# Two chunks' keys as a seven-product pair, and the loads reordered to suit, in a gated attention + GEGLU kernel

## The chip, the cores and the metric

The kernel runs on one core of one Trainium2 chip. The metric is the device time of one execution in microseconds (us). Engines are named as in the profile: PE is TensorE's matmul stream, PEld its weight loads, DVE is VectorE, ACT is ScalarE, POOL is GpSimd, SP is SyncE, which here only issues DMA transfers.

## The reference, cut to what matters

```python
# x: 2048 x 1024, wqkv: 1024 x 3072, wo: 1024 x 1024, w_gate and w_up: 1024 x 3584, w_down: 3584 x 1024, bf16
qkv = x @ wqkv                                  # 32 heads of 32
# every row attends to itself and 7 rows behind it, 2 apart
a = softmax(q . k[rows] / sqrt(32)) @ v[rows] @ wo
b = (gelu(x @ w_gate) * (x @ w_up)) @ w_down
g = sigmoid((x * gate_w).sum(-1))
out = g * a + (1 - g) * b
```

## The kernel before: the parts that matter here

The 2048 rows are four chunks of 512. Chunks 0 and 1 are the first half (`sup == 0`), chunks 2 and 3 the second. Each half does queries, keys and values, then the feed-forward network (FFN), then the two down projections. The attention of a half runs on DVE while PE is in the FFN.

Most products are "seven-product pairs", a Strassen-like scheme: a 2 x 2 block product takes seven block matmuls instead of eight. DVE pays for it with sums and differences of weight blocks ("forms") and with additions behind the products. In the kernel before, of the first half's queries, keys and values only the values are such a pair. Queries and keys of chunks 0 and 1 are plain: eight tiles of eight matmuls per chunk.

```python
def main():                                     # the order of work on PE
    ...                                         # transposes of chunk 0's input
    yield from qkv_outer(0)                     # queries of chunk 0
    yield from qkv(0, 1)                        # keys of chunk 0
    yield from gate(0)
    yield from qkv_pair(0, [2])                 # values of chunks 0 and 1: seven products
    yield from gate_sum(0)
    yield from qkv(1, 0)                        # queries of chunk 1
    yield from qkv(1, 1)                        # keys of chunk 1
    yield from gate(1)
    yield from halo(1)
    for sup in range(NSUP):
        ...                                     # ffn, down, then the second half's pair

def loads():                                    # the order of loads, all issued by SP
    ...                                         # query weights, eight loads
    yield from load_qkv(0, 1, range(KT))        # key weights
    yield Op("SP", ...)                         # value weights
    yield from load_x(1, [])                    # chunk 1's input, eight transposing loads
    yield load_prep(0)                          # blocks of w_down for the down projection's forms
    yield load_prep(2)
    yield from load_block(0, 0)                 # FFN weights
    ...
```

The order of instructions on each engine is fixed while the program is written. A planner holds a modelled clock per engine and one for the DMA pipe, and always emits next the operation that its model can start first. Each stream of operations has a bias, and some operations have a due time before which the bias counts.

```python
class Weave:
    LAT = 0.1
    RATE = 340e3                                # bytes per us
    AHEAD = 11.0
    ...
    def _emit(self, op, t):
        ...
        if op.eng in ("SP", "POOL", "ACTQ"):    # a DMA
            nbytes, issue = op.cost
            self.clk[self.home(op)] = t + issue
            self.pipe = max(self.pipe, t) + nbytes / self.RATE
            op.end = self.pipe + 2.2 + ...
        else:
            self.clk[op.eng] = t + cost
    ...
            b = s[0] if op.due is None or t + self.AHEAD < op.due else 0.0
            if best is None or t + b < best[0]:
                best = (t + b, t, s, op)

w.run([(0.0, main()), (0.0, loads()), (0.0, late_x()), (0.88, wforms()), (0.0, down_forms()), (0.1, x_forms()),
       (1.43, qkv_forms()), (1.3, preps()), (0.13, attention()), (0.36, scores())])
```

Every DMA byte costs the planner the same, whatever the size of the packets it travels in.

Of the kernel before, what the change touches and what calls it, by code (L numbers as in the profile page):

```python
# [30 lines left out]
class Op:  # L31


    def __init__(self, eng, cost, fn, deps=(), key=None, table=None, pre=None, lag=0.0, tail=0.08, kind=None, after=False, due=None):
        self.eng, self.cost, self.fn, self.deps, self.key = eng, cost, fn, deps, key
        self.table, self.pre, self.lag, self.tail = table, pre, lag, tail
        self.kind = kind
        self.after, self.ins = after, None
        self.due = due
        self.end = None  # L40


class Weave:
# [7 lines left out]
    AHEAD = 11.0  # L51
# [76 lines left out]
    def run(self, streams):  # L128
# [5 lines left out]
        while live:  # L134
            best = None
            for s in live:
                op = s[2] if isinstance(s[2], Op) else s[2]()
                t = None if op is None else self._start(op)
                if t is None:
                    continue  # L140
                b = s[0] if op.due is None or t + self.AHEAD < op.due else 0.0
                if best is None or t + b < best[0]:
                    best = (t + b, t, s, op)
# [9 lines left out]
def kernel(  # L153
# [63 lines left out]
    DUE = (88.5, 308.0)  # L217
# [33 lines left out]
    def bank_take():  # L251
        best = min(range(len(bank_free)), key=lambda i: -1.0 if bank_free[i][1] is None else bank_free[i][1].end)
        return bank_free.pop(best)

    def bank_give(i, op):
        bank_free.append((i, op))

# [37 lines left out]
    warm = hrow[:, XR + NST, 0:SC]  # L295
    nc.vector.memset(warm, 0.0)
    for i in range(5):
        nc.tensor.matmul(banks[7][:], lhsT=warm[:, 0:P], rhs=warm, start=True, stop=True)
# [27 lines left out]
    def load_qkv(c, which, order=range(KT), deps=()):  # L326
        for kt in order:
            yield ring_load(("wqkv", c, which, kt), lambda g, kt=kt: nc.sync.dma_start(
                out=g.rearrange("p (k n) -> p k n", k=1), in_=qkv_src(which, kt, 1)), deps)

# [60 lines left out]
    def loads():  # L391
        for kt in range(KT):
            yield Op("SP", (P * D * 2, 0.45), lambda kt=kt: nc.sync.dma_start(
                out=qbuf[:, kt:kt + 1], in_=qkv_src(0, kt, 1)), key=("wqkv", 0, 0, kt))
        yield from load_qkv(0, 1, range(KT))
        yield Op("SP", (KT * P * D * 2, 1.0), lambda: [nc.sync.dma_start(out=vbuf[:, hf * KH:(hf + 1) * KH],
                                                                        in_=qkv_src(2, hf * KH, KH)) for hf in range(2)],
                 [("pt", NST - 1, 1)], key=("wqkv", 0, 2))
        yield from load_x(1, [])
# [24 lines left out]
    def preps():  # L424
        for i0 in range(0, NPREP, 2):
# [5 lines left out]
            f0 = dve(t, lambda: V(out=b11, in0=b12, in1=b11, op=ALU.subtract), due=DUE[0] + 4.0 * i0, deps=[("prep", i0), ], lag=1.0)  # L431
            yield f0
            yield dve(t, lambda: V(out=b12, in0=b22, in1=b12, op=ALU.subtract), due=DUE[0] + 4.0 * i0)  # L433
            f1 = dve(t, lambda: V(out=b22, in0=b22, in1=b11, op=ALU.subtract), [f0], due=DUE[0] + 4.0 * i0)
            yield f1
            last = dve(t, lambda: V(out=b21, in0=b21, in1=b22, op=ALU.subtract), [f1], due=DUE[0] + 4.0 * i0)
# [33 lines left out]
    def x_forms():  # L470
        t = tt(KH * SC)
        for sup in range(NSUP):
# [4 lines left out]
            t1 = dve(t, lambda b12=b12, b11=b11: V(out=tf[:, 0], in0=b12, in1=b11, op=ALU.subtract), dx + free, lag=1.0, key=("xf", sup, 1))  # L477
            yield t1
            t2 = dve(t, lambda b22=b22: V(out=tf[:, 1], in0=b22, in1=tf[:, 0], op=ALU.subtract), [t1], key=("xf", sup, 2))
            yield t2  # L480
            yield dve(t, lambda b12=b12, b22=b22: V(out=b12, in0=b22, in1=b12, op=ALU.subtract), [("z", c0)], key=("xf", sup, 3))  # L481
            yield dve(t, lambda b21=b21: V(out=tf[:, 2], in0=b21, in1=tf[:, 1], op=ALU.subtract), [t2], key=("xf", sup))
# [22 lines left out]
    def qkv(c, which):  # L505
# [3 lines left out]
        for t in range(NT):  # L509
# [11 lines left out]
        if c == 1 and which == 1:  # L521
            for kt in range(KT):
                ring_give(("wqkv", 0, 1, kt), o)

    def qkv_outer(c):
        taken = [bank_take() for t in range(NT)]
        for kt in range(KT):
# [8 lines left out]
            else:  # L536
                o = pe(NT, go, d)
                yield o
        for t in range(NT):
            i = taken[t][0]  # L540
            if t % 2 == 0 or c:
# [11 lines left out]
    def qkv_forms():  # L553
        for sup in range(NSUP):
            c = 2 * sup
            t = tt(D // 2)
            for which in QVK if sup else (2,):
                def raw(kt, hi, which=which, c=c):
                    return qkv_w(c, which, kt).rearrange("p (m t) -> p m t", t=NT)[:, :, KH * hi:KH * hi + KH]

                def form(f, kt, which=which, c=c):
                    return ring[:, held["wqf", c, which, f, kt // 2], kt % 2 * D // 2:(kt % 2 + 1) * D // 2] \
                        .rearrange("p (m t) -> p m t", t=KH)

                for f in range(4):
                    for kt in range(KH):
                        if True:
                            def go(f=f, kt=kt, which=which, c=c):
                                if f != 2 and kt % 2 == 0:
                                    ring_take(("wqf", c, which, f, kt // 2))  # L570
                                o, x_, y_, op = ((lambda: form(0, kt), lambda: raw(kt, 1), lambda: raw(kt + KH, 1), ALU.add),
                                                 (lambda: form(1, kt), lambda: form(0, kt), lambda: raw(kt, 0), ALU.subtract),
                                                 (lambda: raw(kt, 1), lambda: raw(kt, 0), lambda: raw(kt, 1), ALU.subtract),
                                                 (lambda: form(3, kt), lambda: raw(kt + KH, 0), lambda: form(1, kt),
                                                  ALU.subtract))[f]
                                V(out=o(), in0=x_(), in1=y_(), op=op)  # L576
                            dep = raw_keys(c, which, (kt, kt + KH))
                            if f in (1, 2):
                                dep.append(("wq", c, which, 0, kt))
                            elif f == 3:  # L580
                                dep.append(("wq", c, which, 1, kt))
                            yield dve(t, go, dep, key=("wq", c, which, f, kt), lag=0.5,
                                      pre=ring_pre if (f != 2 and kt % 2 == 0) else None,
                                      due=DUE[1] + 23.0 * QVK.index(which) + 2.5 * f if sup else 0.0)
# [20 lines left out]
    def qkv_pair(c, whichs=QVK):  # L605
# [35 lines left out]
        for which in whichs:  # L641
            for g in range(2):
                ts = (2 * g, 2 * g + 1)
                A, Bk, Dk, m5, u2 = {}, {}, {}, {}, {}
                for t in ts:
# [3 lines left out]
                    Bk[t], fr = bank_take()  # L649
# [103 lines left out]
    def gate_sum(c):  # L753
# [13 lines left out]
        bank_give(i, e)  # L767
# [14 lines left out]
    def scores():  # L782

        for c in range(NCH):
            q_, k_ = qo[c % 2], kT[c]
            for a in range(SC // AC):
# [15 lines left out]
                def add(t):  # L802
                    def fn():
                        V(out=w3(box[0]), in0=w3(box[0]), in1=w3(box[t]), op=ALU.add)  # L804
                    return dve(tt(n), fn, [last["m", t], last["acc"]], key=("qk", h) if t == NT - 1 else None, kind="a")

                todo, pend = list(range(NT)), []
# [27 lines left out]
    def att_half(c, a, h):  # L835
# [112 lines left out]
        def s4(t):  # L948
            return flat(("s", t // 2)).rearrange("p (u w s) -> p u w s", u=2, w=4)

        def sums(t, m):
            def fn():
                V(out=s4(t)[:, t % 2], in0=w3(box["p", t])[:, 0:4], in1=w3(box["p", t])[:, 4:8], op=ALU.add)  # L953
            return dve(tt(n // 2), taking(("s", t // 2), fn) if t % 2 == 0 else fn, [m],
                       pre=xb_pre() if t % 2 == 0 else None)
# [9 lines left out]
        for t in range(0, NT + 2, 2):  # L965
            for u in range(2):
# [3 lines left out]
                if t:  # L970
                    if u == 0:
                        f = fold2(t - 2, [ss[t - 2], ss[t - 1]])
                        yield f
                    else:
                        f = fold1(t - 2, f)
                        yield f
                        xb_give(box["s", (t - 2) // 2], f)
                        if a and t == NT:
                            w.done["att", c] = f
            if t < NT:  # L980
                for u in range(2):
                    ss[t + u] = sums(t + u, ms[t + u])
                    yield ss[t + u]
                    xb_give(box["p", t + u], ss[t + u])
# [3 lines left out]
    def ffn(sup, mid, early=()):  # L988
# [29 lines left out]
        for i in range(FT + 2):  # L1018
            if i < FT:
# [3 lines left out]
                Bk[f], fr = bank_take()  # L1023
# [303 lines left out]
```

## Time and profile before

| before | value | from |
|---|---|---|
| time, median | 725.16 us | timed runs |
| span of the profiled execution | 723.8 us | page, first line |
| PE busy | 713.6 us, 99% | page, part 1 |
| DVE busy | 598.5 us, 83% | page, part 1 |
| DVE busy from 40 to 300 us | 246.57 us, 94.8% | windows |
| waits of PE, in sum | about 3 us | waits of PE |

The head of the page of before: the span, and each engine's busy time with its share of the span and its number of instructions.

```profile
span 723.8 us, 9915 instructions
...
PE 713.6 (99%) x3314; PEld 351.1 (49%) x3381; DVE 598.5 (83%) x898; ACT 315.3 (44%) x535; POOL 71.8 (10%) x128
```

The waits of PE in before: what waited, what it waited for, us in total, times, longest.

```profile
PE ps L298 <- DVE hT L296: 1.2, 1, 1.2
PE ps L1252 <- DMA hT<-in_A_x_dram: 0.5, 1, 0.5
PE ps L628 <- DVE lend L481: 0.5, 1, 0.5
PE ps L995 <- ACT m L1049: 0.4, 1, 0.4
PE ps L496 <- DVE lend L1259: 0.3, 1, 0.3
```

PE is full. The first wait is before the real work starts. From the first query matmul on, PE stands for about 1 us in the whole kernel. So this kernel gets faster only if PE gets less to do, or by that 1 us.

The timeline of PE in before, at the borders of the stages: start, length, operation, and in brackets an idle time ahead of it with its releaser.

```profile
7.02 13.97 PE L496 MATMUL ps<-lend,hT 128*128 128x512 bf16 x62 [0.29 <-DVE lend L1259]
...
88.11 1.04 PE L995 MATMUL ps<-lend,ring 128*128 128x512 bf16 x4
...
312.65 1.05 PE L735 MATMUL ps<-lend,gcol 128*32 128x512 bf16 x16
...
441.66 1.03 PE L995 MATMUL ps<-lend,ring 128*128 128x512 bf16 x4
```

These are four clock readings: queries start at 7.02, the first FFN at 88.11, the second half's gates at 312.65, the second FFN at 441.66. Their differences are the stage lengths.

### The profile page before, as it was taken

Reading aid. Unit: us, or ns where it says so; the run is one execution under the profiler, and the core shown is the slowest. Engines: PE = TensorE matmul, PEld = TensorE weight load, DVE = VectorE, ACT = ScalarE, POOL = GpSimd, SP = SyncE. Lnnn points to the kernel's source line nnn. Section 1 sums busy time; section 2 is a strip of 40 time slices with the busy share of each in tenths; the row PEclk is TensorE's granted clock in tenths of the full one; section 3 lists DMA queues with packets and bytes.
Section 4 is the critical chain, followed back from the end, with each engine's and each line's share of the span. In section 5 each row is a group of like instructions: output and inputs, shape, how many; then the busy total and the mean of one; then the engine's idle time right before and its main releaser. Section 6 shows DMA issues by size and latency. Waiting matters only on the chain.

```text
span 723.8 us, 9915 instructions
## 1 busy us (share of the span) xinstructions
PE 713.6 (99%) x3314; PEld 351.1 (49%) x3381; DVE 598.5 (83%) x898; ACT 315.3 (44%) x535; POOL 71.8 (10%) x128
## 2 busy tenths in 40 slices
PE   8999999999999999999999999999999999999997
PEld 5666644444444444455665444444444444444443
DVE  1799999999999899799599976999999995794200
ACT  2353465557655532035552114567558557110110
POOL 1000433343121100100000000000000000001000
PEclk9999999999999999999999999999999999999999
DMA  9944799989989979945239999786566657999992
GB/s 313 236 149 103 222 354 318 334 256 349 267 218 193 274 239 299 344 143 146 58 97 300 362 324 309 236 186 177 157 178 159 177 157 178 313 326 331 327 304 99
DMA packets 180931, 172.12 MB, mean 238 GB/s; under 512 B 56464, under 2 KB 137360, under 8 KB 180880
## 3 DMA queue, kind: packets, MB, share of 16 engines
q1 hardware_dynamic: 172048, 143.69, 68.5%
q0 software_dynamic: 8544, 27.27, 10.7%
q8 instruction: 26, 0.43, 0.2%
q10 hardware_dynamic: 288, 0.52, 0.2%
q14 instruction: 25, 0.20, 0.1%
HBM read 129.50 MB, written 28.31 MB: 218 GB/s over the span
## 4 chain that ended last, share of the span: by engine, by line
PE 83%; DVE 8%; DMA 4%; issue 4%; POOL 1%; ACT 0%; DVEq 0%; POOLq 0%; ACTq 0%
PE ps L995 35%; PE ps L1159 28%; PE ps L628 12%; PE ps L496 8%; DMA fforms<-ring 1%; DVE ring L457 1%; DVE ring L576 1%; DVE hT L1058 1%; DMA ring<-in_B_w_down_dram 1%; DMA ring<-in_A_wqkv_dram 1%; DMA hT<-in_A_wo_dram 1%; DMA hT<-in_B_w_down_dram 1%; DVE hT L1120 1%; DVE hT L1039 1%; DVE hT L433 0%
## 5 line engine op out<-in xcount | busy, mean ns | idle before, releaser
L995 PEld LDWEIGHTS <-ring 128*128 128x128 bf16 x1568 | 153.2, 98 | 185.8 <-issue 1.6
L995 PE MATMUL ps<-lend,ring 128*128 128x512 bf16 x877 | 210.5, 379 | 1.3 <-ACT m L1049 0.4
L995 PE MATMUL ps<-tf,ring 128*128 128x512 bf16 x659 | 162.6, 379 | 0.7
L1159 PE MATMUL ps<-ring,hT 128*128 128x512 bf16 x696 | 159.7, 379 | 0.6
L1159 PEld LDWEIGHTS <-hT 128*128 128x128 bf16 x708 | 69.2, 98 | 83.3
L945 DVE TENSOR_TENSOR xbuf<-xbuf,lend 128x2048 bf16<-128x2048 bf16 x64 | 77.4, 1215 | 7.5 <-DMA xbuf<-xbuf 7.5
L798 DVE TENSOR_TENSOR xbuf<-qo,lend 128x2048 bf16<-128x2048 bf16 x64 | 76.7, 1216 | 0.1
L804 DVE TENSOR_TENSOR xbuf<-xbuf 128x2048 bf16<-128x2048 bf16 x56 | 68.2, 1217 | 0.3
L628 PEld LDWEIGHTS <-ring 128*128 128x128 bf16 x384 | 49.3, 129 | 34.4 <-DVE lend L481 0.9
L1024 ACT COPY ps<-ps 128x512 f32<-128x512 f32 x56 | 32.0, 571 | 55.6 <-PE ps L995 55.5
L1067 ACT ACTIVATE gl<-ps 128x512 bf16<-128x512 f32 x56 | 33.5, 598 | 49.6 <-PE ps L995 48.5
L1194 ACT ACTIVATE ost<-ps,omg 128x512 bf16<-128x512 f32 x16 | 11.0, 688 | 100.6 <-PE ps L1159 81.9
L1186 POOL DMA_DIRECT2D out_dram<-ost x24 | 13.0, 540 | 411.0 <-ACT ost L1194 319.1
L1159 PE MATMUL ps<-ring,qo 128*128 128x512 bf16 x187 | 48.5, 379 | 0.2
L466 POOL DMA_DIRECT2D fforms<-ring x56 | 30.6, 546 | 175.3 <-DVE ring L457 166.1
L628 PE MATMUL ps<-lend,ring 128*128 128x512 bf16 x203 | 47.0, 380 | 0.7 <-DVE lend L481 0.5
L1039 DVE TENSOR_TENSOR hT<-hT,gl 128x1024 bf16<-128x1024 bf16 x56 | 38.3, 683 | 11.3 <-ACT hT L1036 11.3
L953 DVE TENSOR_TENSOR xbuf<-xbuf 128x1024 bf16<-128x1024 bf16 x64 | 42.0, 683 | 0.4
L1079 DVE TENSOR_TENSOR u<-ps,u 128x512 f32<-128x512 f32 x56 | 38.3, 684 | 4.6 <-PE ps L995 3.2
L628 PE MATMUL ps<-tf,ring 128*128 128x512 bf16 x173 | 40.1, 379 | 0.2
L1058 DVE TENSOR_TENSOR hT<-ps,m 128x512 bf16<-128x512 f32 x56 | 38.2, 683 | 1.5 <-PE ps L995 1.4
L1075 ACT COPY u<-ps 128x512 f32<-128x512 f32 x56 | 32.9, 587 | 15.1 <-PE ps L995 15.1
(110 smaller groups left out, 697.1 us busy)
## 6 DMA issues: line engine op xcount, KB each, us to landing
ring<-dforms SPq DMA_DIRECT2D x112, 256.0 KB, 5.3
ring<-in_B_w_down_dram SPq DMA_DIRECT2D x84, 256.0 KB, 4.6
ring<-in_B_w_gate_dram SPq DMA_DIRECT2D x56, 256.0 KB, 4.8
fforms<-ring POOLq DMA_DIRECT2D x56, 256.0 KB, 5.3
ring<-fforms SPq DMA_DIRECT2D x56, 256.0 KB, 4.0
ring<-in_B_w_up_dram SPq DMA_DIRECT2D x42, 256.0 KB, 4.7
ring<-in_A_wqkv_dram SPq DMA_DIRECT2D x32, 256.0 KB, 5.4
ring<-oforms SPq DMA_DIRECT2D x32, 256.0 KB, 5.7
```

The lines of the kernel that those rows point to most:

```text
L496: nc.tensor.matmul(banks[bk][:], lhsT=lhsT, rhs=xT(c, kt), start=(kt == 0), stop=(kt == KT - 1))
L628: nc.tensor.matmul(banks[bk][:], lhsT=lhsT, rhs=rhs[:, kt, :], start=(start and kt == 0), stop=(kt == KH - 1), skip_group_check=True)
L798: V(out=w3(box[t]), in0=q_b, in1=k_w, op=ALU.mult)
L804: V(out=w3(box[0]), in0=w3(box[0]), in1=w3(box[t]), op=ALU.add)
L945: return dve(tt(n), taking(("p", t), lambda: V(out=w3(box["p", t]), in0=w3(box["ab"]), in1=v_w, op=ALU.mult)), [("qkv", c, 2, t), abo] + ( ...
L953: V(out=s4(t)[:, t % 2], in0=w3(box["p", t])[:, 0:4], in1=w3(box["p", t])[:, 4:8], op=ALU.add)
L995: nc.tensor.matmul(banks[bk][:], lhsT=wv[:, k, fl * P:(fl + 1) * P], rhs=rhs[:, k, :], start=(start and k == 0), stop=(k == KH - 1), skip_ ...
L1039: yield dve(tt(2 * SC), lambda f=f: nc.vector.tensor_tensor(out=hrow[:, f, :], in0=hrow[:, f, :], in1=gl[f][:], op=ALU.mult), [e, ev[f, "g ...
L1058: ev[f, "up2"] = dve(tt(SC, True), lambda f=f: nc.vector.tensor_tensor(out=hs(f, 1), in0=v3(banks[Bk[f]][:]), in1=v3(m5[f][:]), op=ALU.add ...
L1067: nc.scalar.activation(out=gl[f][:, SC:2 * SC], in_=banks[A[f]][:], func=ACT.Gelu_apprx_tanh)
L1079: e = dve(tt(SC, True), lambda f=f: nc.vector.tensor_tensor(out=u2[f][:], in0=banks[Dk[f]][:], in1=u2[f][:], op=ALU.add), [o, ev[f, "u2"]])
L1159: nc.tensor.matmul(banks[bk][:], lhsT=l, rhs=wv[:, i, :], start=(start and k == 0), stop=(q == last and i == 1), skip_group_check=True)
```

## The change

The intent: keys of chunks 0 and 1 also become a seven-product pair, which takes 16 of 128 matmuls away. A pair needs the input of both chunks, so chunk 1's input is wanted sooner. Three query tiles of chunk 1 are put ahead of the pair, to give the key weights time to land. Chunk 1's transposing loads are issued from ACT's queue, the key weights from POOL behind the sixth of them, and the value weights last. With this went a retuned planner (due times, biases), forms and attention sums merged into fewer, wider instructions, a longer warm-up and some smaller changes (input forms that wait for half of the loads, the order of score sums, the choice of PSUM banks). The core of the diff:

```diff
-    AHEAD = 11.0
+    AHEAD = 17.53
...
+    NFILL = 3
-    DUE = (88.5, 308.0)
+    DUE = (99.8, 308.54)
...
-    for i in range(5):
-        nc.tensor.matmul(banks[7][:], lhsT=warm[:, 0:P], rhs=warm, start=True, stop=True)
+    for n_ in [SC] * 6 + [P] * 3:
+        nc.tensor.matmul(banks[7][:, 0:n_], ...)
...
+    def early_x():                              # chunk 1's input, issued from ACT's queue
+        for kt in range(KT):
+            yield Op("ACTQ", (P * SC * 2, 1.3), lambda kt=kt: nc.scalar.dma_start_transpose(
+                out=xT(1, kt), in_=x[SC:2 * SC, kt * P:(kt + 1) * P]), [("pt", NST - 1, 1)], key=("x", 1, kt))
+    def early_k():                              # key weights, issued from POOL after x(1, 5)
...
     def loads():
-        yield from load_qkv(0, 1, range(KT))
-        yield from load_x(1, [])
...
     def preps():                                # forms of the down weights; prep block i0
-            f0 = dve(..., due=DUE[0] + 4.0 * i0, ...)
+            f0 = dve(..., due=DUE[0] + 4.84 * i0, ...)
...
     def qkv_forms():                            # one instruction now takes two weight rows
-            t = tt(D // 2)
-            for which in QVK if sup else (2,):
+            t = tt(D)
+            for which in QVK if sup else (1, 2):
                 def raw(kt, hi, which=which, c=c):
-                    return qkv_w(c, which, kt).rearrange("p (m t) -> p m t", t=NT)[:, :, KH * hi:KH * hi + KH]
+                    w0, w1 = qkv_w(c, which, kt), qkv_w(c, which, kt + 1)
+                    return _win_ap(w0[:, KH * hi:KH * hi + 1], [[w1.offset - w0.offset, 2], [NT, P], [1, KH]])
...
     def main():
         yield from qkv_outer(0)
-        yield from qkv(0, 1)
         yield from gate(0)
+        yield from gate(1)
+        yield from qkv(1, 0, range(0, NFILL))
+        yield from qkv_pair(0, [1])
+        yield from gate_sum(0)
+        yield from gate_sum(1)
         yield from qkv_pair(0, [2])
-        yield from gate_sum(0)
-        yield from qkv(1, 0)
-        yield from qkv(1, 1)
-        yield from gate(1)
+        yield from qkv(1, 0, range(NFILL, NT))
         yield from halo(1)
...
-    w.run([..., (0.88, wforms()), ..., (1.43, qkv_forms()), (1.3, preps()), (0.13, attention()), (0.36, scores())])
+    w.run([..., (0, wforms()), ..., (0, qkv_forms()), (0.85, preps()), (0.11, attention()), (0.24, scores())])
```

## The prediction

> **What bounds the kernel now.** TensorE: the page gives PE 99% of 723.8 us, and the waits view lists 3 us of PE waits in all. Neighbouring 512-column matmuls start 215.8 ns apart in the timeline (64 query matmuls from 7.02 to 20.83 us). The Trainium skill, "TensorE: Matmul & The Clock Gate", section "Wait — 56ns, not 53.3ns?", gives 215.7 ns for a warm one; the trace agrees. From 7.02 us to the last matmul start at 719.7, everything above that pace sums to about 1 us. DVE is 83% busy overall, but 94 to 99% from 30 to 310 us (windows), so it is the engine to watch.
>
> **Removed.** Keys of chunks 0 and 1 cost 2 x 64 matmuls; as a seven-product pair, 7 x 4 tiles x 4 = 112. 16 matmuls x 0.2158 = 3.45 us leave TensorE's gap-free path. FFN, down projections and the second half keep their counts.
>
> **Added and moved.**
> - DVE: eight key forms (0.60 us each) and eight PSUM adds (0.6 each). Given back: 16 value forms of 0.335 become 8 of 0.60, as in the second half; 64 attention sums of 0.60 become 32 of about 1.13. Net about +5 us, +7 before 270 us.
> - Chunk-0 scores start near 38 us instead of 32.7. Chunk-1 attention ends at 231 us now and is needed only near 390, so it can slide.
> - Start: the first real matmul waits 0.3 us for a DVE copy; reordered transposes gain 0.1 to 0.3 us. The longer warm-up hides behind the input's landing (4.0 us).
> - Loads: chunk 1's eight transposing loads (1.3 us apart at best) start near 7.4 us beside the query weights, which alone land until 12.5. I estimate their landing at 20 to 21.5; the gate of chunk 1 needs them at 21.4. Key weights follow the sixth; eight loads landed 0.67 us apart before, so I estimate 27 to 28. Three query tiles (24 x 0.2158 = 5.2 us) carry PE to 27.2; the first form's product needs all key weights plus 1.3 us of DVE by 28.9. Both hand-overs are within 1 us of late: I allow 0.7 us of stalls here, 0.2 elsewhere.
>
> **Time.** 725.16 - 3.45 - 0.2 + 0.9 = 722.4 us; 8 in 10 between 720.8 and 724.6. Either 2% would need 14.5 us, four times what leaves PE: faster 1%, same 98%, slower 1%.
>
> **What would show it.**
> - A key block of 24.2 us of matmuls after about 27 us; FFN's first matmul near 85 us (88.1 before), later by whatever PE stalled.
> - PE waits: at most one of about 1 us before the second gate (transposing loads) and one in the key pair (weights or their forms).
> - DVE over 94% between 40 and 300 us with PE waits near zero there; chunk-1 attention ending some us after 231.
> - Last matmul to the end: unchanged 4 us.
>
> **What would make it wrong.** If the transposing loads are served late (the first ones took 8 to 11 us behind the value weights), gate and key pair stall 3 us or more and the gain is gone. Or DVE falls behind with FFN's weight forms, or with the stores that must finish before the upper rows of the hidden tile are written (about 181 us). Or loads issued from ACT delay its copies out of PSUM near 20 us and PE waits for banks.

## More of the kernel before

DVE is the engine to watch in the FFN. It is not the bottleneck there, but it is nearly full and it feeds PE, so any time in which it stands can't be made up quickly. The waits of DVE from 40 to 265 us in before, longest first; three shorter ones, all for PE, are cut:

```profile
DVE u L1079 <- PE ps L995: 2.2, 2, 2.0
DVE hT L1039 <- ACT hT L1036: 1.9, 2, 1.2
...
```

It waits for PE and for ACT, and in this stretch never for a DMA.

## The result, and the profile after

After the change the median is 726.92 us (726.11 to 729.26, four runs). Before has 725.58 us (725.13 to 726.19, four runs). The ratio is 1.0023, with a 95% interval from 0.9998 to 1.0048. A ratio here is always the mean time of one kernel's fast runs over that of the other's in the same rounds, so it is not quite the ratio of the medians quoted. The class "within 2%" was right. The time was not: 726.9 us against a predicted 722.4, and outside the range of 720.8 to 724.6.

The head of the page of after:

```profile
span 725.0 us, 9844 instructions
...
PE 712.6 (98%) x3302; PEld 348.7 (48%) x3369; DVE 600.6 (83%) x849; ACT 315.5 (44%) x540; POOL 75.9 (10%) x136
```

The counts of PE can't be compared: the profile of the same kernel run again (r1 below) has 3369 matmuls, so some records are missing here, and in before too.

The waits of PE in after:

```profile
PE ps L651 <- DVE qo L712: 1.5, 1, 1.5
PE ps L1018 <- ACT m L1072: 1.0, 3, 0.6
PE ps L309 <- DVE xbuf L307: 0.9, 1, 0.9
PE ps L758 <- DMA lend<-in_A_x_dram: 0.7, 1, 0.7
...
```

The timeline of PE in after, at the same borders and at two waits:

```profile
7.57 13.97 PE L518 MATMUL ps<-lend,hT 128*128 128x512 bf16 x62 [0.17 <-ACT lend L1288]
...
23.21 0.38 PE L758 MATMUL ps<-lend,gcol 128*32 128x512 bf16 x1 [0.70 <-DMA lend<-in_A_x_dram]
...
86.14 1.03 PE L1018 MATMUL ps<-lend,ring 128*128 128x512 bf16 x4
...
312.35 1.05 PE L758 MATMUL ps<-lend,gcol 128*32 128x512 bf16 x16
...
325.95 1.89 PE L651 MATMUL ps<-tf,ring 128*128 128x512 bf16 x8 [1.50 <-DVE qo L712]
...
442.85 1.03 PE L1018 MATMUL ps<-lend,ring 128*128 128x512 bf16 x4
```

The differences of these readings give the stage lengths. The last two columns belong to experiments told below.

| stage, us | before | after | after, again (r1) | r6 | r10 |
|---|---|---|---|---|---|
| start to the first query matmul | 7.02 | 7.57 | 6.87 | 7.26 | 6.59 |
| queries, keys, values of the first half | 81.09 | 78.57 | 77.99 | 77.53 | 78.28 |
| first FFN and its first down projection | 224.54 | 226.21 | 228.13 | 223.91 | 224.57 |
| second half's gates and pairs, second down projection | 129.01 | 130.50 | 130.30 | 129.39 | 128.30 |
| second FFN to the last matmul | 278.04 | 278.04 | 278.04 | 278.04 | 277.86 |
| after the last matmul started | 4.1 | 4.1 | 4.1 | 3.8 | 4.1 |

The gain is there. The first stage is 2.52 us shorter: 3.45 us of matmuls are gone, and the two gates take 0.95 us longer from start to start than in before, 0.70 us of it the listed wait (-3.45 + 0.95 = -2.50). Then it is given back: 0.55 us at the start, 1.67 us in the FFN (1.91, counting a gate's sum of 0.24 us that moved out of it into the first stage, where it runs together with the other one), and 1.49 us in the second half's pairs. In sum -2.52 + 0.55 + 1.67 + 1.49 = +1.19 us, which is the difference of the spans.

The waits of DVE in after, from 40 to 265 us:

```profile
DVE ring L479 <- DMA ring<-in_B_w_up_dram: 2.9, 2, 2.4
DVE xbuf L968 <- DMA xbuf<-xbuf: 1.2, 1, 1.2
...
```

Now DVE waits for DMAs in this stretch, 4.3 us in sum with a small third wait that is not shown. In before it waited for none there. The timeline of DVE in after shows the largest such wait, and another one outside that stretch:

```profile
131.00 0.69 DVE L1081 TENSOR_TENSOR hT<-ps,m 128x512 bf16<-128x512 f32 x1
134.08 0.69 DVE L479 TENSOR_TENSOR ring<-ring 128x1024 bf16<-128x1024 bf16 x1 [2.38 <-DMA ring<-in_B_w_up_dram]
...
309.89 0.69 DVE L596 TENSOR_TENSOR ring<-ring 128x1024 bf16<-128x1024 bf16 x1 [1.27 <-DMA ring<-in_A_wqkv_dram]
```

The first is an FFN weight form whose weights were issued at 121.33 us and landed at 133.985, 12.7 us later. Comparable loads in before, issued at 121.4, took 4.7 us. The windows of both kernels: window, length, busy time of PE, PEld, DVE, ACT and POOL with counts, PE's clock, the DMA share, GB/s. A packet's whole time is counted in the window where it starts, and packets overlap, so the share can pass 1. Before:

```profile
80.00:105.00 25.00, 24.75 (x126) 12.55 (x128) 23.88 (x34) 13.61 (x24) 10.24 (x17) 1.00 1.02 316
105.00:135.00 30.00, 29.88 (x137) 13.59 (x139) 29.83 (x48) 16.84 (x30) 11.71 (x19) 1.00 0.97 332
```

After:

```profile
80.00:105.00 25.00, 24.79 (x114) 12.51 (x116) 24.55 (x48) 15.64 (x30) 6.89 (x11) 1.00 0.65 215
105.00:135.00 30.00, 29.89 (x138) 13.58 (x140) 27.58 (x40) 16.41 (x29) 12.41 (x19) 1.00 1.08 339
```

Both kernels move 172.12 MB in the whole execution, but after leaves a third of the DMA idle from 80 to 105 us and is somewhat fuller than before in the next 30 us. The share alone is not the cause: it stands at 1.07 there in r10 below too, where DVE waits for no load. The down-weight blocks did not move between these stretches either, although their forms have a later due time (99.8 us instead of 88.5, then 4.84 us a step instead of 4): both kernels issue eight such loads in each. What is new from 105 to 135 us is two transposes of chunk 0's attention. SP reaches them at 108.68 and 114.72 us in after, and in before at 75.42 and 80.60. SP issues in the order of its program, and it stands twice. From 96.4 to 103.2 us it waits for the buffers of the down-weight blocks, which must be stored first; from 108.7 it waits for ACT, which makes what the first transpose reads. Two lines in the waits of SP's DMA queue in after, 100 to 125 us:

```profile
...
SPq L379 <- DMA dforms<-hT: 7.9, 3, 6.8
SPq L959 <- ACT u L1098: 5.3, 1, 5.3
...
```

The second transpose went out at 116.5 us. Four down-weight loads and three FFN loads followed between 117.2 and 122 us, and from 115 to 120 us the DMA share was 1.25 at only 211 GB/s. In before seven such loads were issued from 114.2 to 122.3 us with no transpose near. That the transposes made the loads late is a reading of these traces; no run moved them alone.

The lines of FFN weights in the DMA view of 118 to 136 us (transfer, queue, kind, number, KB each, median us to landing) in after:

```profile
...
ring<-in_B_w_up_dram SPq DMA_DIRECT2D x4, 256.0 KB, 8.9
ring<-in_B_w_gate_dram SPq DMA_DIRECT2D x3, 256.0 KB, 12.7
```

The same view of before:

```profile
...
ring<-in_B_w_up_dram SPq DMA_DIRECT2D x4, 256.0 KB, 5.2
...
ring<-in_B_w_gate_dram SPq DMA_DIRECT2D x3, 256.0 KB, 5.2
```

How a wait of DVE becomes a wait of PE can be followed step by step in the second profile of the same kernel (run r1 below), where the wait is longer. The timelines of DVE, ACT and PE in r1 around 135 us, put in one fence:

```profile
133.58 0.69 DVE L479 TENSOR_TENSOR ring<-ring 128x1024 bf16<-128x1024 bf16 x1 [3.16 <-DMA ring<-in_B_w_up_dram]
...
134.79 0.68 DVE L1102 TENSOR_TENSOR u<-ps,u 128x512 f32<-128x512 f32 x1
...
135.51 0.63 ACT L1106 ACTIVATE gl<-u 128x512 bf16<-128x512 f32 x1 [2.97 <-DVE u L1102]
...
136.51 0.59 ACT L1072 COPY m<-ps 128x512 f32<-128x512 f32 x1
...
137.15 1.89 PE L1018 MATMUL ps<-lend,ring 128*128 128x512 bf16 x8 [0.96 <-ACT m L1072]
```

The late weights hold up a form at the head of DVE's queue. Behind it, after one more form, stands `u`, which has nothing to do with these weights, and it comes 3 us late. ACT waits 2.97 us for `u`. The copy `m` stands behind that on ACT, and PE waits 0.96 us for `m`. Two thirds of the delay were slack; the rest reaches PE. The Trainium skill, "Perfetto Trace Analysis", section "Tensor Engine Instruction (MATMUL, LD_WEIGHTS)", says of the other engines that "ACT/DVE/GPSIMD are strict FIFO". The trace agrees: two engines stood 3 us with ready work behind the head of the queue.

Four theories were then on the table:

- **T1, late DMAs in the FFN:** the new order makes loads collide, DVE waits for them, and PE pays for part of it. Suspects are the down-weight blocks near 105 to 135 us, and the transposing loads of chunks 2 and 3 (187 to 203 us), beside which attention's own transposes now fall. These are issued at 202.95 us in after; in before they were issued at 181.35, ahead of those loads.
- **T2, DVE too full:** the change gives DVE more to do, and it falls behind by its own work.
- **T3, merged forms in the second half:** an instruction that reads two weight rows waits for more loads than it needs.
- **T4, the start:** the first stage differs from one execution to the next.

### The profile page after: what moved, and what is told of

Same layout as the page of the kernel before. It is cut to its first block, busy times and chain, and to the rows that moved or that the text cites. A ratio compares the mean times of both kernels' runs of the same rounds, so it can differ in the third digit from the quotient of the medians.

```text
span 725.0 us, 9844 instructions
## 1 busy us (share of the span) xinstructions
PE 712.6 (98%) x3302; PEld 348.7 (48%) x3369; DVE 600.6 (83%) x849; ACT 315.5 (44%) x540; POOL 75.9 (10%) x136
## 2 busy tenths in 40 slices
DMA packets 180419, 172.12 MB, mean 237 GB/s; under 512 B 56464, under 2 KB 137360, under 8 KB 180368
## 4 chain that ended last, share of the span: by engine, by line
PE 73%; DMA 8%; issue 7%; DVE 5%; POOL 3%; ACTq 1%; ACT 1%; SPq 0%; POOLq 0%; DVEq 0%
PE ps L1018 28%; PE ps L1183 28%; PE ps L651 15%; PE ps L518 2%; POOL dforms L463 1%; DMA xbuf<-xbuf 1%; DMA ring<-in_B_w_up_dram 1%; POOL fforms L488 1%; ACTq L345 1%; DMA dforms<-hT 1%; DMA hT<-in_A_wqkv_dram 1%; DMA hT<-in_B_w_down_dram 1%; DMA ring<-oforms 1%; DVE xbuf L968 1%; DMA lend<-in_A_x_dram 1%
## 5 line engine op out<-in xcount | busy, mean ns | idle before, releaser
L1018 PEld LDWEIGHTS <-ring 128*128 128x128 bf16 x1568 | 153.4, 98 | 187.8 <-issue 4.0
L1018 PE MATMUL ps<-lend,ring 128*128 128x512 bf16 x878 | 210.7, 379 | 2.3 <-ACT m L1072 1.0
L1018 PE MATMUL ps<-tf,ring 128*128 128x512 bf16 x658 | 162.4, 379 | 0.8
L651 PEld LDWEIGHTS <-ring 128*128 128x128 bf16 x496 | 63.9, 129 | 45.4 <-issue 2.6
L827 DVE TENSOR_TENSOR xbuf<-xbuf 128x2048 bf16<-128x2048 bf16 x56 | 68.3, 1220 | 0.2
L651 PE MATMUL ps<-lend,ring 128*128 128x512 bf16 x269 | 61.8, 379 | 0.6 <-ACT u2q L695 0.3
L651 PE MATMUL ps<-tf,ring 128*128 128x512 bf16 x216 | 50.4, 379 | 1.8 <-DVE qo L712 1.5
L1106 ACT ACTIVATE gl<-u 128x512 bf16<-128x512 f32 x56 | 35.4, 633 | 32.5 <-DVE u L1102 32.2
L479 DVE TENSOR_TENSOR ring<-ring 128x1024 bf16<-128x1024 bf16 x56 | 37.9, 686 | 3.0 <-DMA ring<-in_B_w_up_dram 2.9
L978 DVE TENSOR_TENSOR xbuf<-xbuf 128x2048 bf16<-128x2048 bf16 x32 | 39.1, 1223 | 0.1
```

Of the source, the lines that this page charges most:

```text
L479: nc.vector.tensor_tensor(out=g, in0=ring[:, held[("w", 0, b, x_)], :], in1=ring[:, held[("w", 0, b, y_)], :], op=op)
L651: nc.tensor.matmul(banks[bk][:], lhsT=lhsT, rhs=rhs[:, kt, :], start=(start and kt == 0), stop=(kt == KH - 1), skip_group_check=True)
L827: V(out=w3(box[0]), in0=w3(box[0]), in1=w3(box[t]), op=ALU.add)
L978: V(out=p0.rearrange("p (u n) -> p u n", u=2), in0=lo, in1=hi, op=ALU.add)
L1018: nc.tensor.matmul(banks[bk][:], lhsT=wv[:, k, fl * P:(fl + 1) * P], rhs=rhs[:, k, :], start=(start and k == 0), stop=(k == KH - 1), skip_ ...
L1106: ev[f, "g2"] = act(0.54, lambda f=f: nc.scalar.activation(out=gl[f][:, 0:SC], in_=u2[f][:], func=ACT.Gelu_apprx_tanh), [e], table="gelu")
```

## The experiments

Twelve runs were made. Each was profiled once and timed over 3 rounds (r1 and r12 over 5).

| run | what it is | median (range), us | ratio to before (95%) |
|---|---|---|---|
| r1_again | after, unchanged | 727.48 (726.51 to 731.58) | 1.0033 (1.0015 to 1.0050) |
| r2_half_prep | half of most down-weight loads left out | 725.72 (724.78 to 726.29) | 0.9996 (0.9982 to 1.0011) |
| r3_light_scores | half of chunk 1's score work left out | 727.90 (726.01 to 729.46) | 1.0030 (1.0016 to 1.0043) |
| r4_split_forms | first forms of the second half split | 725.93 (725.17 to 726.78) | 1.0004 (0.9991 to 1.0017) |
| r5_no_late_x | transposing loads of chunks 2, 3 left out | 726.20 (724.92 to 726.45) | 1.0003 (0.9986 to 1.0019) |
| r6_relief_all | r2, r4 and r5 together | 722.34 (721.70 to 723.28) | 0.9956 (0.9941 to 0.9971) |
| r7_split_gate | r4, and the second gate later | 724.66 (724.05 to 725.27) | 0.9987 (0.9972 to 1.0002) |
| r8_replan | r7, DMA repriced in the planner | 724.25 (723.31 to 725.10) | 0.9981 (0.9966 to 0.9996) |
| r9_replanA | r7, other prices | 726.58 (725.28 to 727.72) | 1.0013 (0.9996 to 1.0031) |
| r10_replanB | r7, other prices | 721.55 (721.31 to 721.88) | 0.9942 (0.9928 to 0.9957) |
| r11_replanC | r7, other prices | 725.30 (724.48 to 725.90) | 0.9993 (0.9978 to 1.0008) |
| r12_replanB_again | r10, unchanged | 721.90 (721.74 to 722.13) | 0.9948 (0.9934 to 0.9961) |

The medians of before in these calls lay between 725.56 and 725.85 us.

### r1_again: the changed kernel once more

No edit; five rounds.

> The changed kernel unmodified, run again, for its spread. If the late full clock of its first profile (full speed 6.9 us after the start, 5.6 in the kernel before) is chance, this profile has another time for it, and the first query matmul starts earlier when the clock comes earlier. If the longer warm-up itself delays the clock, it comes at 6.9 again. The four stalls of the first profile (before the second gate 0.7 us, FFN tiles 8 to 10 about 0.85, FFN near 190 to 200 us about 1.2, first key/query pair of the second half 1.5) should come again within 0.5 us each if they belong to the program; time 726 to 728.

Measured: 727.48 us, ratio 1.0033. After is slower than before by a third of a per cent, with an interval that leaves out 1. In its profile the gate's wait is gone and the start is 0.7 us sooner, but the FFN takes 228.13 us, 1.9 more than in the first profile. The waits of DVE from 40 to 265 us in r1:

```profile
DVE ring L479 <- DMA ring<-in_B_w_up_dram: 3.2, 1, 3.2
DVE xbuf L968 <- DMA xbuf<-xbuf: 2.9, 1, 2.9
...
```

What follows: the DMA waits recur on the same two operations, larger than at first, and PE's wait for `m` grew from 1.0 to 2.6 us in sum. So "within 0.5 us each" held only for the wait of 1.5 us in the second half. The 0.7 us wait of the gate in the first profile is not what costs.

### r2_half_prep: less traffic from the down-weight blocks

```diff
-                for k in range(n):
+                for k in range(1 if i0 >= 2 * NSTG else n):
                     nc.sync.dma_start(out=st[:, 2 * h + k], in_=v[:, k])
```

Half of each such load is left out from the fourth block on, so the result is wrong. Instructions on the engines and their order stay.

> Only half of the rows of the down-projection blocks are loaded from the fourth block on (wrong result on purpose); order of all instructions and all DVE work unchanged. Theory DMA (an FFN weight load takes 12 us because the DMA engines are crowded, and VectorE waits 2.4 us for it at 134 us): the wait falls under 1 us, FFN's loss against the kernel before shrinks by 1 to 2 us, time about 725. Rival VectorE (too much added work there): FFN's loss stays within 0.3 us, time about 727.

Measured: 725.72 us, 1.8 us below r1, and the intervals of the ratios don't overlap. In the profile the wait on FFN weights went from one of 3.2 us to three of 1.1 or less (2.5 in sum), two waits of 2.4 us in sum came up on attention's transposes, and the FFN took 226.47 us, against 226.21 and 228.13. What follows: T1 holds for this traffic as far as the timed runs go, at 1.2 us (against the median of after's first runs) to 1.8 (against r1's). It does not say that these blocks had moved (they had not, see above), only that fewer of their bytes give the time back. The profile alone would not carry it: the wait expected to fall under 1 us fell to 1.1, and the FFN lies within the spread of after's two; r4's below has no wait at 134 us at all with the same loads in that stretch.

### r3_light_scores: less work for DVE

```diff
-                        V(out=w3(box[t]), in0=q_b, in1=k_w, op=ALU.mult)
+                        nw = NWIN // 2 if c == 1 else NWIN
+                        V(out=w3(box[t])[:, 0:nw], in0=q_b[:, 0:nw], in1=_win_ap(..., [[-DIL, nw], [1, AC]]), op=ALU.mult)
...
-                        V(out=w3(box[0]), in0=w3(box[0]), in1=w3(box[t]), op=ALU.add)
+                        V(out=w3(box[0])[:, 0:nw], in0=w3(box[0])[:, 0:nw], in1=w3(box[t])[:, 0:nw], op=ALU.add)
```

Half of chunk 1's score products and sums are left out: 683 ns instead of 1216 ns each. The result is wrong; the comparison with the reference doesn't notice it within its tolerance.

> Score products and sums of chunk 1 at half width (wrong result on purpose), about 18 us less VectorE work from 150 us on; order unchanged. Rival VectorE: FFN's whole loss goes and the 1.5 us stall in the second half's first pair too; time about 723.5. Theory DMA: the wait at 134 us and the loss at tiles 8 to 10 stay (0.85 us), since they come before the lightened work; the stall near 190 to 200 us goes, since VectorE makes up its lag there; time about 725.5.

Measured: 727.90 us, the same as after. The waits of DVE from 40 to 265 us in r3:

```profile
DVE ring L479 <- DMA ring<-in_B_w_up_dram: 4.7, 3, 3.7
...
DVE xbuf L970 <- DMA xbuf<-xbuf: 3.3, 1, 3.3
...
```

The lightened work starts at 184.9 us, so the wait of 3.7 us at 134 us comes before it and says nothing of T2. What follows: behind 185 us T2 falls. With less to do, DVE waited there for FFN weights (0.8 us at 191 us, 0.65 at 203) and 3.3 us for attention's transposes, where r1 has 2.9, and no time was gained. The DMA theory's 725.5 us was missed as well. For the loss near 134 us T2 is tested by r6.

### r4_split_forms: the second half's first forms in two instructions

```diff
+                            if sup and f == 0:
+                                for u in range(2):
+                                    wa, wb = [qkv_w(c, which, kt + u + h).rearrange(...)[:, :, KH:2 * KH] for h in (0, KH)]
+                                    V(out=form(0, kt)[:, u], in0=wa, in1=wb, op=op)
+                                return
```

The result is correct. In after, the merged first form reads four weight loads. The compiled program's list of waits for it names all eight semaphores that SP's DMAs use in turn:

```
L596 TensorTensor ring<-ring 128x1024 [waits DMAHW4,5,3,6,2,7,1,0]
```

Seven of these waits are for query-weight loads; the one on DMAHW1 is for an earlier transfer. The trace agrees: the fourth of the loads that it reads landed at 307.58 us, and the instruction started at 309.89, right after the seventh load landed (309.87) and before the eighth did (310.51).

> In the second half the first of the four weight forms is made again in two instructions, one per row block, as before the change; nothing else. Theory: the doubled instruction reaches over ring slots that it does not read and so waits for all eight query-weight loads; split, VectorE's 1.3 us wait near 309 us goes and TensorE's 1.5 us stall in that pair shrinks to under 0.5; time about 725.5. Rival (VectorE is simply late by then from the FFN): the stall stays at 1.2 us or more; time about 727.

Measured: 725.93 us, 1.5 below r1, though the intervals of the ratios just overlap. The timeline of DVE in r4 shows the split forms, and that of PE the wait that they end:

```profile
308.62 0.75 DVE L600 TENSOR_TENSOR ring<-ring 128x512 bf16<-128x512 bf16 x2
...
324.81 1.89 PE L657 MATMUL ps<-tf,ring 128*128 128x512 bf16 x8 [0.87 <-DVE qo L718]
```

The first form runs at 308.62 us without a wait, and PE's wait fell from 1.50 to 0.87 us, not under 0.5 as expected. The stage of the second half's pairs took 129.32 us, against 130.50 and 130.30 in the two profiles of after and 129.01 in before. This is no chance of one profile: in all five with the merged form (after, r1, r2, r3, r5) the stage took 130.28 to 131.03 us, and in the three with after's order and the split (r4, r6, r7) 129.13 to 129.38. What follows: T3 holds, at about 1.0 to 1.2 us.

### r5_no_late_x: without the transposing loads of chunks 2 and 3

```diff
-            yield Op("SP", (P * SC * 2, 1.6), lambda kt=kt: nc.sync.dma_start_transpose(
-                out=xT(c, kt), in_=x[c * SC:(c + 1) * SC, kt * P:(kt + 1) * P]), deps, key=("x", c, kt))
+            yield Op("SP", (P * SC * 2, 1.6), lambda: None, deps, key=("x", c, kt))
```

The result is wrong: chunks 2 and 3 compute on what lies there.

> The sixteen transposing loads of chunks 2 and 3, issued between 187 and 208 us in the changed kernel, are left out (wrong result on purpose); order of everything else unchanged. Theory DMA: attention's own transposes, which slid about 20 us later into these loads, land sooner; VectorE's waits of 1.2 to 3.3 us at 187 to 214 us go, FFN's later loss (after 185 us) shrinks by 1 to 2 us, the earlier one at tiles 8 to 10 stays; time 725 to 726. Rival VectorE: no change, 727.

Measured: 726.20 us, 1.3 below r1 and just above the band expected; the intervals of the ratios overlap. The waits of DVE from 40 to 265 us in r5 are two lines:

```profile
DVE ring L478 <- DMA ring<-in_B_w_up_dram: 3.3, 1, 3.3
DVE hT L1080 <- PE ps L1017: 0.2, 1, 0.2
```

The FFN took 226.83 us, between the two profiles of after. What follows: the later wait, on attention's transposes, is gone, and the earlier one stayed. So these are two collisions, not one. What the later one costs is not settled by this run alone.

### r6_relief_all: the three reliefs together

The edits of r2, r4 and r5. Its output is wrong, which doesn't matter for the time. DVE has as much to do as in after: 251.25 us busy from 40 to 300 us, against 249.18.

> All three reliefs at once: half of the down-projection rows not loaded, chunk 2 and 3 transposing loads left out, first forms of the second half split (wrong result on purpose). Theory DMA: nearly the whole expected gain shows, since what ate it was VectorE waiting for late transfers: time 722 to 723.5, FFN's loss under 0.7 us, the pair's under 0.7. If something else eats it, time stays above 724.5.

Measured: 722.34 us, ratio 0.9956. The waits of DVE from 40 to 265 us in r6, and the timeline of PE at two borders:

```profile
DVE hT L1067 <- ACT hT L1064: 2.4, 2, 1.9
DVE hT L1086 <- PE ps L1023: 0.2, 1, 0.2
```

```profile
84.79 1.03 PE L1023 MATMUL ps<-lend,ring 128*128 128x512 bf16 x4
...
308.70 1.05 PE L763 MATMUL ps<-lend,gcol 128*32 128x512 bf16 x16
```

No wait for a DMA is left in that stretch, PE's timeline lists no wait between these two readings, and the FFN takes 223.91 us, less than in before. What follows: the change saves what was predicted (722.4 us) once these three causes are away. T1 and T3 together account for the loss, and T2 is refuted, now with no less work on DVE. That less traffic would speed any kernel is no rival: the 224.54 us of the FFN in before hold a gate's sum of about 0.24 and a wait of 0.37, so there was hardly more to gain there.

### r7_split_gate: a correct kernel with two small edits

```diff
         yield from gate(0)
-        yield from gate(1)
         yield from qkv(1, 0, range(0, NFILL))
+        yield from gate(1)
         yield from qkv_pair(0, [1])
```

with the split of r4. The gate then comes 24 matmuls (5.2 us) later, and its loads have that much more time.

> Right result: first forms of the second half split, and the gate of chunk 1 after the three query tiles instead of before. Theory: 1.2 us from the split as in the run before; the swap gives nothing in most runs (only one of five profiles showed a wait there, 0.7 us) and takes nothing: time 725.3 to 726.2. If the split's 1.2 us was chance, 727.

Measured: 724.66 us, ratio 0.9987, with an interval that just holds 1. The result is correct. It is 1.3 us below r4 (725.93), but the intervals of the ratios overlap, and the first stage, where the gate is, took 77.82 us here against 77.49 in r4. The time is below the range expected (725.3). What follows: no gain can be put down to the gate's place. Whether r7 really beats r4 stays open.

### r8_replan, r9_replanA, r10_replanB, r11_replanC: the planner told what DMAs cost

The records of DMA packets in the trace of before give the price that the planner's single rate hides. A packet of 256 B, as the transposing loads use, takes one of the 16 engines 25.8 ns on average. One of 512 B takes 29.0, one of 2048 B 97.8, one of 4096 B 181 ns. Over 16 engines that is 159, 283, 335 and 362 GB/s (for 256 B: 256 / 25.8 x 16). As packets overlap, these are estimates to compare with one another: from 24 to 26 us of before, nearly all of it transposing packets, 182 GB/s were moved at a DMA share of 0.89. The planner prices all at 340. So transposing loads are 340 / 159 = 2.1 times as dear as planned. In the four runs they are priced higher, sometimes the FFN blocks too, and the planner's due times and biases are set anew for these prices, by a search in the planner's own model. That model orders candidates; its times are no forecast of the chip's, which is why several went to the chip. The edit, with the values of r10:

```diff
-    AHEAD = 17.53
+    AHEAD = 8.63
-    XB = 9                                      # FFN block behind which chunk 2's input is loaded
+    XB = 10
-    DUE = (99.8, 308.54)
+    DUE = (126.59, 236.04)
...
-            yield Op("ACTQ", (P * SC * 2, 1.3), lambda kt=kt: nc.scalar.dma_start_transpose(
+            yield Op("ACTQ", (P * SC * 2 * 2.1, 1.3), lambda kt=kt: nc.scalar.dma_start_transpose(
...                                              # the same for load_x and attention's transposes
-    ... due=DUE[0] + 4.84 * i0                  # down-weight forms
+    ... due=88.21 + 6.067 * i0
...
-    w.run([..., (0, wforms()), ..., (0, qkv_forms()), (0.85, preps()), (0.11, attention()), (0.24, scores())])
+    w.run([..., (0.015, wforms()), ..., (10.617, qkv_forms()), (0.311, preps()), (0.05, attention()), (0.255, scores())])
```

| run | transposes priced | FFN blocks priced | latency, us |
|---|---|---|---|
| r8 | x 2.1 | x 1.15 | 2.5 |
| r9 | x 2.1 | x 1.15 | 2.2 |
| r10 | x 2.1 | x 1.0 | 2.2 |
| r11 | x 1.8 | x 1.1 | 2.3 |

> Right result: as the run before, and the kernel's own planner, which fixes the order of instructions, is told dearer transfers (transposing ones 2.1 times their bytes, FFN weight blocks 1.15 times, 0.3 us more latency) and its due times are set anew for that. Theory DMA: an order made for transfers as slow as they are leaves VectorE few waits on transfers in FFN: time 722 to 724.5, below both kernels. Rival VectorE: VectorE's work is the same, so no better than 726.

Measured: 724.25 us, ratio 0.9981, correct, and within the expected range. The FFN took 224.20 us, as in before, but the second half's pairs took 130.52: PE waited 2.0 us there for a weight form. The repricing mended the stage that it was for and the new order lost time in another.

> Right result, as r8, with another setting of due times, found for the planner with transposes at 2.1 times and FFN weight blocks at 1.15 times their bytes; in its own plan TensorE never stops in FFN nor in the second half's first pair (r8's plan still held the 2 us stop there that its profile shows). Theory DMA: 721.5 to 723. Rival (the rest is chance, r8's FFN was luck): 724.5 or more.

Measured: 726.58 us; the expectation was missed. FFN 225.36 us, second half's pairs 131.43. PE waited 2.9 us in one piece for a weight form of the second half, at 316.7 us.

> As r9 with FFN weight blocks priced at their plain bytes. Theory DMA: transposes alone are priced right, weight blocks a little too cheap; 722 to 724, no better than r9.

Measured: 721.55 us, ratio 0.9942: better than expected, and faster than both kernels, with a correct result. The stage lengths are in the table above. The waits of DVE from 40 to 265 us in r10 begin with

```profile
DVE xbuf L904 <- DMA xbuf<-xbuf: 0.9, 1, 0.9
DVE hT L1068 <- ACT hT L1065: 0.5, 1, 0.5
```

Waits for DMAs in this stretch are 0.9 us, against 4.3 and 6.3 in the two profiles of after. PE's timeline lists one wait between 85 and 437 us, of 0.7 us. DVE is busier than in after (602.7 us of the span against 600.6).

> As r9 with transposes at 1.8 times, weight blocks at 1.1 times. Theory DMA: between, 721.5 to 723.5.

Measured: 725.30 us; missed as r9 was, with the second half's pairs at 130.69 us and two waits of PE for forms there, 1.19 and 0.81 us.

What follows from the four: with the same matmuls and nearly the same DVE work the order alone is worth 5 us, from 721.55 to 726.58. What it is about r10's prices and due times that makes its order hold in the second half where r8, r9 and r11 stalled stays open. In the first FFN all four differ from after alike: SP reaches the two transposes of chunk 0's attention at 96 to 104 us, ahead of the crowded stretch, and at 107 to 115 in after and r1 to r7. One of four is a choice of the best, so it was run again.

### r12_replanB_again: the best one once more

No edit to r10; five rounds.

> The fastest kernel again, for its spread and because it was picked as the best of three. If its order holds: 721 to 722.5 in nearly all runs, no VectorE wait over 1 us between 40 and 260 us, no stall in the second half's first pair. If the first measurement was luck of the DMA's timing: 723 or more, with such waits.

Measured: 721.90 us, ratio 0.9948 (0.9934 to 0.9961). In its profile the longest wait of DVE for a DMA from 40 to 265 us is 0.9 us, and the second half's first pair has no listed wait, as expected of an order that holds. The gain is not the luck of one draw. Against before it is half a per cent, 3.8 us by the medians.

## Why the prediction was right and wrong, point by point

**What bounds the kernel: right.** PE was 99% busy before and 98% after, and nothing but PE's work and PE's waits moved the time.

**"16 matmuls x 0.2158 = 3.45 us leave TensorE's gap-free path": right.** The key pair ran from 28.76 to 53.03 us in the trace of after, 24.27 us, with 24.2 predicted. The first FFN began at 86.14 us in the first profile, and at 84.8 to 85.5 in all twelve that followed, with "near 85 us" predicted. "FFN, down projections and the second half keep their counts" holds too: the second FFN to the last matmul takes 278.04 us in both.

**"I allow 0.7 us of stalls here": right in size for the first profile.** The one wait is 0.70 us at the second gate. Its last transposing load took 5.18 us because key-weight loads were issued from POOL 0.04 us after it; in r4, where they came 1.14 us after it, it took 2.75 us. The Trainium skill, "DMA: Bandwidth & Descriptors", section "Issuing engines are not separate DMA queues", says that transfers from different issuers run on the same 16 engines and interleave; the wait agrees with that. It was gone in r1, whose time is no better.

**The start, "reordered transposes gain 0.1 to 0.3 us": not seen.** The first query matmul came at 7.57 us instead of 7.02, and in the other twelve profiles of the changed kernel and its variants at 6.59 to 7.47. One thing that delays it is when TensorE reaches full speed: neighbouring input transposes on PE start 107 ns apart before that moment and 56 ns after. It came 6.89 us into the execution in after, 5.61 in before, and at 3.57 to 6.89 over the thirteen profiles of the changed kernel and its variants, which all issue the same warm-up. This spread of 3.3 us fits the Trainium skill, "TensorE: Matmul & The Clock Gate", section "What's actually happening", which gives a free-running window of 3413 ns. The longer warm-up didn't make the moment dependable. It is not all: the four latest moments (6.10 to 6.89 us) go with starts of 7.26 to 7.57, but the two earliest (3.57 in r12, 3.81 in r7) go with 7.25 and 7.47, because there PE waited for the first query weights, which landed at 7.21 and 7.42. T4 is thus real, but it is noise of some tenths of a us in the time.

**"0.2 elsewhere" is the step that failed.** The prediction's sum has the terms -3.45, -0.2 and +0.9, the last made of 0.7 of stalls at the hand-overs and "0.2 elsewhere". Elsewhere measured 1.91 us in the FFN and 1.49 us in the second half's pairs in the first profile, 3.4 us in all, and more in the second one. Three assumptions stood behind the 0.2:

- *DVE's extra work as the cost of the forms.* I counted "about +5 us" of DVE work and named "DVE falls behind with FFN's weight forms" as a danger. Measured, DVE's busy time rose by 2.1 us, and the amount was harmless: less of it gained nothing (r3), and more of it ran in 721.55 us (r10). What hurt is the order: a form stands at the head of the queue with its weights not yet there.
- *Loads after the start as free.* I costed the loads of the first 30 us and none behind them. I foresaw that chunk 0's scores would start later, and not that its transposes through the DMA would slide with them. They came into the stretch from 105 to 135 us; SP stood up to 5.3 us at them, the loads behind were issued close together, and FFN weights took up to 12.7 us to land instead of 4.7. Halving the down-weight loads from the fourth block on gave 1.2 to 1.8 us back (r2); the transposes' own part is argued from the traces and not tested.
- *"Chunk-1 attention ends at 231 us now and is needed only near 390, so it can slide."* It did slide: its last fold ran at 231.45 us in before and at 245.63 in after. But its transposes through the DMA slid with it, from 181 us to 203 us, beside the transposing loads of chunks 2 and 3. DVE waited up to 2.9 us for them (r1), and without those loads the wait was gone (r5). Slack in the data does not mean slack in the traffic.

The merged forms were not in the sum at all, except as a saving ("16 value forms of 0.335 become 8 of 0.60, as in the second half"). I read the merge as fewer instructions, and not as a wider dependence: the second half's first form came to wait for seven loads instead of the four that it reads. Undoing it (r4) measured about 1.0 to 1.2 us, of the 1.5 that the second half's pairs lost.

**The planner's view.** The planner's own end for PE's work is 718.93 us for after and 723.63 for before: it expected 4.7 us of gain, with every DMA byte at one price. In before, DVE ran 2 us and more ahead of the plan nearly all along. In after it loses 2.4 us against the plan at 134 us (from 0.9 ahead to 1.5 behind) and 1.3 us at 309.9, at the very waits shown above.

**What stays open.** The cost in the FFN was not split further between the traffic of the down-weight blocks, SP's wait of 6.8 us for their buffers (r2 eases both) and the two transposes at which SP stood. The place of DVE's waits differs from one execution to the next: r4 had none at 134 us and 2.7 us near 188. So the single profiles show the mechanism, and the sizes rest on the timed runs. And what makes r10 the best of four orders is not known beyond its stage times.

## What to carry to other kernels

When a change moves work on a kernel whose instruction order is fixed in advance, cost the DMA traffic of every stage that shifts, not only of the stage that you edit: an engine at 95% that waits 3 us at the head of its queue for a late load takes everything behind it along. Before you merge two instructions into a wider one, look at what the merged one waits for, and not only at what it reads. And a planner that prices all bytes alike doesn't see that some are dear: measure the time of a packet by its size, give that to the planner, and still let the chip choose among several orders.

## What the Trainium skill lacked or had wrong

- "DMA: Bandwidth & Descriptors", section "Latency and other measured facts", gives a transposing DMA 261 GB/s effective with a non-contiguous middle dimension and about 350 to 400 when contiguous. The transposing loads here, in 256-byte packets of 25.8 ns each on one of 16 engines, come to an estimated 159 GB/s from that time, and 182 GB/s were moved in a stretch of 2 us with little else. The price of 2.1 in r8 to r10 rests on it.
- The same page, section "Why small descriptors are slow (HBM only)", puts a descriptor of 256 B at 27% overhead. Here a byte in 256-byte packets took 2.1 times as long as one in 2048-byte packets (25.8 ns / 256 against 97.8 ns / 2048), and in 512-byte packets 1.2 times. The 256-byte packets are the transposing ones, so this run doesn't part the size from the transposing.
- The same page gives latencies, but no figure for how far the landing of a whole transfer moves when one core's own transfers crowd. Here 256 KB of FFN weights, issued at 121.4 us in one kernel and at 121.33 us in the other, took 4.7 us and 12.7 us to land, by what else was under way.
- No page says that a hand-made access pattern across two buffers can make an instruction wait for more loads than it reads: seven waited for, four read, 1.0 to 1.2 us.
- "TensorE: Matmul & The Clock Gate" agreed with the traces in the pace of 512-column matmuls and in the free-running window. But the 500 ns by which it lets the moment of full speed vary to either side is too little here: with the same warm-up it came between 3.57 and 6.89 us over thirteen executions.
